# The first MLP's weight conversions on VectorE: whole tiles of 1024 columns, or halves of 512

## The chip, the cores and the metric

The kernel runs on one core of a Trainium2 chip. The metric is the device time of one execution in microseconds. The kernel before took 947.5 us, the median of three runs (946.28 to 948.18). The profiled execution took 947.39 us, of which the span from its first to its last instruction is 945.7 us.

## The reference

A causal attention over a window of 128 positions (4 sequences of 576 positions, 8 heads of 64, with a linear distance bias), and behind it two MLPs with different activations. All inputs and outputs are float32.

```python
scores = scale * np.matmul(q, k.transpose(0, 1, 3, 2))
rel = pos[:, None] - pos[None, :]
mask = (rel >= 0) & (rel < window)
scores = np.where(mask, scores + slopes * -abs(rel), -1e9)
attn = softmax(scores)
x = np.matmul(attn, v)                     # 2304 tokens x 512
h = x @ w_in1                              # 512 -> 2048
g = np.where(h >= 1, h, np.where(h <= -1, 0.0, (h + 1) ** 2 / 4))
x = g @ w_out1                             # 2048 -> 512
h = x @ w_in2
out = (h * np.clip(h + 3.0, 0.0, 6.0) / 6.0) @ w_out2
```

## The kernel before

Matmuls need more than one pass for float32 accuracy, so each operand is held as two parts, a high one and a low remainder, and each product is three matmuls (low x high, high x low, high x high).

The weights of both MLPs arrive as 64-bit floats. A tile of weights belongs to one slice f of 128 of the 2048 inner columns (f = 0 to 15) and holds, for 128 partitions, 512 columns of w_in and 512 of w_out: 1024 columns. To become float32 high and low parts it passes through six steps on three engines (the class `Weights`):

- `conv1`: ScalarE takes the magnitude of the upper words (line 194, tile `ma`), GpSimd clears what is not the sign in them (line 197, into `rawa`), ScalarE shifts the lower words (line 198, into `rawa`).
- `conv2`: VectorE shifts the magnitude and joins the sign (line 205), then adds the lower words as integers (line 212).
- `conv3`: ScalarE writes the high part (line 152, `wa<-ma`), VectorE the low part (line 159, `wa<-ma,wa`).

For the first MLP that is three VectorE instructions of 1024 columns for each of 16 slices. The names in the instruction order carry the slice: `ma3` and `wa3` belong to f = 3.

The attention runs in units of up to 256 positions, head by head, in steps: scores on TensorE into a bank `s` (line 411), the masked maximum on VectorE (line 441, `sm`), the exponential on ScalarE (line 445), transposes (lines 469, 470), values (line 506), the division on VectorE (lines 518 to 520, `y`), a transpose back (line 531), and the two parts of the MLP's input `x`: the high part on ScalarE (line 152), the low part on VectorE (line 159, `x<-x,x`). `x7` is the last pair of heads of the first unit.

The first MLP works on blocks of tokens: three of 256 and then wider ones of 384. For each slice f it makes `h` (12 matmuls, line 659, into one of two banks), the activation (VectorE line 688, ScalarE line 689, VectorE line 690, which ends the use of the bank), the two parts of `g` (ScalarE line 152, GpSimd line 159), and the second product into `acc` (12 matmuls, line 701), two slices behind. Blocks 0 and 1 go through slices 0 to 7 and then both through 8 to 15, so that the conversions, the loads and the attention's next units can run beside them. The conversions of w_in1 and w_out1 are spread over about the first 126 us. The second MLP has its own conversions (`mb`, `wb`), made around 500 to 570 us.

In this part of the program the order on SyncE (the DMA queue) is the order of the code; that of the four compute engines is set by a scheduler from the dependencies and the order of the code. Each engine then works through its list strictly in order.

Of the kernel before, what the change touches and what calls it, by code (L numbers as in the profile page):

```python
# [12 lines left out]
U32 = mybir.dt.uint32  # L13
I32 = mybir.dt.int32
U16 = mybir.dt.uint16
AF = mybir.ActivationFunctionType
ALU = mybir.AluOpType
# [23 lines left out]
def tile_window_attention_two_mlps(  # L41
# [15 lines left out]
    nc = tc.nc  # L57
# [92 lines left out]
    def split_hi(eng, hi, x):  # L150
        if eng == "act":
            nc.scalar.copy(hi, x)  # L152
        elif eng == "pool":
            nc.gpsimd.tensor_scalar(out=hi, in0=x, scalar1=1.0, scalar2=1.0, op0=ALU.mult, op1=ALU.mult)
        else:
            engines[eng].tensor_copy(hi, x)

    def split_lo(eng, lo, x, hi):
        engines[eng].tensor_tensor(out=lo, in0=x, in1=hi.bitcast(F32), op=ALU.subtract)  # L159
# [3 lines left out]
    class Weights:  # L163
# [36 lines left out]
        def conv2(self, f):  # L200


            raw, m = self.raw[f], self.m[f]
            if self.sign_pool:
                nc.vector.scalar_tensor_tensor(out=m.bitcast(U32), in0=m.bitcast(U32), scalar=3, in1=raw[..., 1],
                                               op0=ALU.logical_shift_left, op1=ALU.bitwise_or)
            else:
                nc.vector.tensor_scalar(out=m.bitcast(U32), in0=m.bitcast(U32), scalar1=3, scalar2=None,
                                        op0=ALU.logical_shift_left)
                nc.vector.scalar_tensor_tensor(out=m.bitcast(U32), in0=raw[..., 1], scalar=0x80000000,  # L210
                                               in1=m.bitcast(U32), op0=ALU.bitwise_and, op1=ALU.bitwise_or)
            nc.vector.tensor_tensor(out=m.bitcast(I32), in0=m.bitcast(I32), in1=raw.bitcast(I32)[..., 0], op=ALU.add)

        def conv3(self, f):
            del self.raw[f]
            m = self.m.pop(f)
            hl = wpool.tile([P, 2, 2, PIECE], F32R, tag=f"w{f}", name=f"w{self.nm}{f}")
            split_hi("act", hl[:, 0], m)
            split_lo("dve", hl[:, 1], m, hl[:, 0])
            self.hl[f] = hl  # L220

        def conv_tick(self):
# [618 lines left out]
    with ExitStack() as actx:  # L841
        mlp1 = Mlp1(W1, blocks1, rpool, gpool)
        raw = actx.enter_context(tc.tile_pool(name="raw", bufs=2))
# [92 lines left out]
    def tail_hook(f):  # L936
        if f >= LAG:

            W2.load()
            W2.load()  # L940
        if 4 <= f < 4 + 2 * KC:
            load_x2(xpool2, xs2, (f - 4) // KC, (f - 4) % KC)
        if f > LAG:
            with tc.issue_after(mlp1.square.ins), tc.issue_after(mlp1.larger.ins):
                conv2(0.5)
# [172 lines left out]
    def pair_hook(f, k):  # L1118
        if f == 0:
            W2.load()  # L1120
            W2.load()
        conv2(0.6)
        n = 2 * f + k
        if n == OWN - 1:
            assert not W2.conv_tick()
            xa.load(0)
            weight_sums(0)
            xa.make(0, temp_a)
            weight_sums(1)
            xa.make(1, temp_a)  # L1130
            weight_sums(2)
        if n == OWN + 3:
            xa.load(1)
        if n >= OWN:
            spare(1.3)
# [205 lines left out]
```

## Time and profile before

| what | value |
|---|---|
| median of 3 runs | 947.5 us |
| profiled execution | 947.39 us, span 945.7 us |
| TensorE busy | 929.6 us (98%) |
| VectorE busy | 661.1 us (70%) |
| ScalarE busy | 534.0 us (56%) |
| GpSimd busy | 305.9 us (32%) |

The shares are means over stages. In the page's row of 40 slices VectorE is at eight or nine tenths up to about 126 us and lower behind that, while TensorE is at nine tenths or more from about 50 us to the end. A busy TensorE is not TensorE at its peak, since its matmuls are pipelined. The granted clock is 1.000 of full speed over the whole span, the level of 2.4 GHz.

### The profile page before, as it was taken

Reading aid. Unit: us, or ns where it says so; the run is one execution under the profiler, and the core shown is the slowest. Engines: PE = TensorE matmul, PEld = TensorE weight load, DVE = VectorE, ACT = ScalarE, POOL = GpSimd, SP = SyncE. Lnnn points to the kernel's source line nnn. Section 1 sums busy time; section 2 is a strip of 40 time slices with the busy share of each in tenths; the row PEclk is TensorE's granted clock in tenths of the full one; section 3 lists DMA queues with packets and bytes.
Section 4 is the critical chain, followed back from the end, with each engine's and each line's share of the span. In section 5 each row is a group of like instructions: output and inputs, shape, how many; then the busy total and the mean of one; then the engine's idle time right before and its main releaser. Section 6 shows DMA issues by size and latency. Waiting matters only on the chain.

```text
span 945.7 us, 17240 instructions
## 1 busy us (share of the span) xinstructions
PE 929.6 (98%) x5683; PEld 875.8 (93%) x5683; DVE 661.1 (70%) x1750; ACT 534.0 (56%) x1349; POOL 305.9 (32%) x575
## 2 busy tenths in 40 slices
PE   8899999999999999999999999999999999999998
PEld 6799999999999999999999999999999898888987
DVE  5998975786677676767645999958557777644443
ACT  6998854676667566666634886535333334423233
POOL 3343854787668676767710000000000000000000
PEclk9999999999999999999999999999999999999999
DMA  9758332222212212222007861004264644544441
GB/s 263 233 168 262 112 99 88 68 81 72 73 54 82 72 52 62 80 84 56 7 34 249 304 235 59 1 23 167 79 211 166 236 170 147 170 124 114 122 113 67
DMA packets 95337, 114.90 MB, mean 122 GB/s; under 512 B 8848, under 2 KB 73616, under 8 KB 95248
## 3 DMA queue, kind: packets, MB, share of 16 engines
q1 hardware_dynamic: 95248, 113.80, 38.4%
q8 instruction: 45, 0.74, 0.3%
q14 instruction: 44, 0.36, 0.1%
HBM read 88.60 MB, written 25.17 MB: 120 GB/s over the span
## 4 chain that ended last, share of the span: by engine, by line
PE 86%; DVE 6%; DMA 3%; ACT 2%; issue 2%; POOL 0%; SPq 0%; ACTq 0%; POOLq 0%; DVEq 0%
PE h L659 25%; PE acc L760 21%; PE acc L701 17%; PE y L1242 7%; PE x L1242 5%; PE s L411 4%; PE r L554 3%; PE t L470 2%; PE r L506 1%; DMA rawa<-w_in 1%; DMA x2r<-x2d 1%; DVE r L688 1%; DMA kw<-kT 1%; DVE x L159 1%; DVE r L690 1%
## 5 line engine op out<-in xcount | busy, mean ns | idle before, releaser
L659 PE MATMUL h<-x,wa 128*128 128x384 f32 (+1 forms) x1344 | 231.0, 317 | 1.2 <-DVE r L690 0.8
L701 PE MATMUL acc<-g,wa 128*128 128x384 f32 (+1 forms) x1344 | 227.4, 315 | 0.4 <-POOL g L159 0.4
L760 PE MATMUL acc<-wb,g 128*128 128x512 f32 x861 | 222.2, 393 | 0.0
L659 PEld LDWEIGHTS h<-x,wa 128*128 128x128 f32 x1344 | 206.6, 189 | 4.4 <-DVE r L690 3.2
L701 PEld LDWEIGHTS acc<-g,wa 128*128 128x128 f32 x1344 | 206.2, 189 | 0.7 <-POOL g L159 0.6
L760 PEld LDWEIGHTS acc<-wb,g 128*128 128x128 f32 x861 | 159.4, 188 | 24.9
L152 ACT CAST g<-r 128x384 fp32r<-128x384 f32 (+1 forms) x208 | 101.3, 487 | 70.9 <-DVE r L1189 37.6
L159 POOL TENSOR_TENSOR g<-r,g 128x256 fp32r<-128x256 f32 (+1 forms) x96 | 92.9, 968 | 67.4 <-ACT g L152 54.3
L689 ACT ACTIVATE r<-r 128x384 f32<-128x384 f32 (+1 forms) x112 | 53.3, 478 | 82.9 <-DVE r L688 82.6
L159 DVE TENSOR_TENSOR g<-r,g 128x384 fp32r<-128x384 f32 x112 | 62.3, 557 | 41.9 <-ACT g L152 41.7
L688 DVE TENSOR_SCALAR r<-h 128x384 f32<-128x384 f32 (+1 forms) x112 | 55.4, 495 | 47.3 <-PE h L659 40.5
L488 POOL TENSOR_SCALAR_AFFINE_SELECT tt<-dist 128x256 fp32r<-128x256 f32 (+1 forms) x176 | 76.8, 457 | 14.1 <-DVE dist L483 13.9
L690 DVE TENSOR_TENSOR r<-h,r 128x384 f32<-128x384 f32 (+1 forms) x112 | 55.7, 499 | 29.7 <-ACT r L689 27.9
L659 PE MATMUL h<-x,wb 128*128 128x384 f32 x384 | 72.6, 336 | 0.0
L659 PEld LDWEIGHTS h<-x,wb 128*128 128x128 f32 x384 | 68.2, 188 | 2.6
L445 ACT ACTIVATE p<-p,sm 128x128 f32<-128x128 f32 (+2 forms) x134 | 56.9, 426 | 21.9 <-DVE sm L441 21.6
L1187 ACT ACTIVATE r<-u 128x384 f32<-128x384 f32 x32 | 16.8, 525 | 56.2 <-DVE u L1251 56.2
L554 PEld LDWEIGHTS r<-tt,vs 128*128 128x128 f32 x304 | 44.7, 189 | 3.5 <-issue 1.3
L393 POOL TENSOR_TENSOR qs<-qr,qs 128x256 fp32r<-128x256 f32 (+2 forms) x64 | 39.3, 616 | 25.0 <-ACT qs L390 13.3
L554 PE MATMUL r<-tt,vs 128*128 128x128 f32 (+3 forms) x304 | 44.3, 262 | 1.7 <-POOL tt L488 0.9
L391 DVE SCALAR_TENSOR_TENSOR kl<-kr,kh 128x256 fp32r<-128x256 f32 (+3 forms) x64 | 39.2, 613 | 0.0
L470 PE MATMUL t<-ident,p 128*128 128x128 f32 x134 | 38.4, 288 | 0.5 <-ACT tt L152 0.5
(161 smaller groups left out, 1554.3 us busy)
## 6 DMA issues: line engine op xcount, KB each, us to landing
w<-wd SPq DMA_DIRECT2D x88, 256.0 KB, 2.7
rawa<-w_in SPq DMA_DIRECT2D x16, 512.0 KB, 5.2
rawa<-w_out SPq DMA_DIRECT2D x16, 512.0 KB, 5.6
rawb<-w_in SPq DMA_DIRECT2D x16, 512.0 KB, 3.8
rawb<-w_out SPq DMA_DIRECT2D x16, 512.0 KB, 4.7
wd<-sum SPq DMA_DIRECT2D x32, 256.0 KB, 2.1
wd<-wb SPq DMA_DIRECT2D x24, 256.0 KB, 2.8
out<-o SPq DMA_DIRECT2D x17, 256.0 KB, 2.3
```

What stands on the lines that cost most here:

```text
L152: nc.scalar.copy(hi, x)
L159: engines[eng].tensor_tensor(out=lo, in0=x, in1=hi.bitcast(F32), op=ALU.subtract)
L445: nc.scalar.activation(out=pt[:, :nk], in_=pt[:, :nk], func=AF.Exp, bias=sm[:, 0:1], scale=-1.0, accum_out=None if u.whole else sm[:, 1:2])
L470: nc.tensor.transpose(ps[:, 1, :], pt[:, P:] if u.whole and has_prev else pt[:, :P], ident)
L488: nc.gpsimd.affine_select(out=u.tt[:, :, s0 + s, :m], in_=both, compare_op=ALU.is_ge, fill=0.0, base=-1 + s, pattern=[[0, 2], [sign, m]], ...
L554: nc.tensor.matmul(u.r[:, qo:qo + nq], u.vs[:, j, c, :, :].rearrange("p a d -> p (a d)"), u.tt[:, part].rearrange("p s q -> p (s q)")[:, s ...
L659: nc.tensor.matmul(ps[:, :n], self.W.w_in(a, c, f), self.x_chunk(x, b, c, n), start=(k == 0), stop=(k == 3 * KC - 1))
L688: nc.vector.tensor_scalar(out=r[:, :n], in0=ps[:, :n], scalar1=-1.0, scalar2=1.0, op0=ALU.max, op1=ALU.min)
L690: self.larger = nc.vector.tensor_tensor(out=r[:, :n], in0=ps[:, :n], in1=r[:, :n], op=ALU.max)
L701: nc.tensor.matmul(acc[i][:, o * n:(o + 1) * n], self.W.w_out(a, f)[:, e * P:(e + 1) * P], g[:, b, :n], start=(first and k == 0 and o == 0 ...
L760: nc.tensor.matmul(acc[t][:, :DM], g[:, b, tg * P:(tg + 1) * P], self.W.w_out(a, f), start=(first and k == 0), stop=(last and k == 2))
L1242: nc.tensor.matmul(ps[:, :N2], w[:, a, c * P:(c + 1) * P], self.x.operand(k, c, b), start=(start and n == 0), stop=(n == 5), skip_group_ch ...
```

## The change

For the first MLP (`sign_pool` is true for it alone) the three VectorE instructions of a slice become six: each works on 512 columns, k = 0 on the w_in half, k = 1 on the w_out half. The shift and the integer addition of one half stand next to each other in the code. ScalarE's and GpSimd's steps stay whole. The second MLP's conversions stay as they were (the branch is only turned round). Blocks, loads and the order of the DMA queue are the same, and 48 instructions are added in all.

```diff
             raw, m = self.raw[f], self.m[f]
             if self.sign_pool:
-                nc.vector.scalar_tensor_tensor(out=m.bitcast(U32), in0=m.bitcast(U32), scalar=3, in1=raw[..., 1],
-                                               op0=ALU.logical_shift_left, op1=ALU.bitwise_or)
-            else:
...
+                for k in range(2):
+                    nc.vector.scalar_tensor_tensor(out=m.bitcast(U32)[:, k], in0=m.bitcast(U32)[:, k], scalar=3,
+                                                   in1=raw[:, k, :, 1], op0=ALU.logical_shift_left, op1=ALU.bitwise_or)
+                    nc.vector.tensor_tensor(out=m.bitcast(I32)[:, k], in0=m.bitcast(I32)[:, k],
+                                            in1=raw.bitcast(I32)[:, k, :, 0], op=ALU.add)
+                return
...
             split_hi("act", hl[:, 0], m)
-            split_lo("dve", hl[:, 1], m, hl[:, 0])
+            if self.sign_pool:
+                for k in range(2):
+                    split_lo("dve", hl[:, 1, k], m[:, k], hl[:, 0, k])
+            else:
+                split_lo("dve", hl[:, 1], m, hl[:, 0])
```

In the changed kernel line 205 has become 206, line 212 has become 208, and lines from 222 on are 7 higher (688 is 695, 690 is 697, 441 is 448, 411 is 418, 659 is 666, 701 is 708, 520 is 527).

VectorE around the last input of the first block (`x7`), before; `r` is the activation of the first slice, `sm9_1` and `sm10_0` are maxima of the attention's second unit:

```order
L520 TENSOR_TENSOR y7_446<-r6_409,rec7_445 128x256
L441 ISA p1_114,sm9_1_489<-s9_1_487,dist_97 128x256
L441 ISA sm9_1_489 128x1
L205 SCALAR_TENSOR_TENSOR ma3_497<-ma3_497,rawa3_329 128x1024
L159 TENSOR_TENSOR x_78<-x7_475,x_78 128x256
L159 TENSOR_TENSOR wa2_494<-ma2_471,wa2_494 128x1024
L688 TENSOR_SCALAR r_514<-h_501 128x256
L212 ISA ma3_497<-rawa3_329,ma3_497 128x2048
L441 ISA p2_115,sm10_0_540<-s10_0_538,dist_97 128x256
```

The same place in the changed kernel:

```order
L527 TENSOR_TENSOR y7_449<-r6_412,rec7_448 128x256
L159 TENSOR_TENSOR wa1_473<-ma1_403,wa1_473 128x512 x2
L448 ISA p1_114,sm9_1_495<-s9_1_493,dist_97 128x256
L448 ISA sm9_1_495 128x1
L159 TENSOR_TENSOR x_78<-x7_481,x_78 128x256
L206 SCALAR_TENSOR_TENSOR ma2_477<-ma2_477,rawa2_261 128x512
L695 TENSOR_SCALAR r_523<-h_510 128x256
L208 ISA ma2_477<-rawa2_261,ma2_477 128x1024
L697 TENSOR_TENSOR r_523<-h_510,r_523 128x256
L206 SCALAR_TENSOR_TENSOR ma3_506<-ma3_506,rawa3_329 128x512 x2
L159 TENSOR_TENSOR wa2_502<-ma2_477,wa2_502 128x512 x2
L208 ISA ma3_506<-rawa3_329,ma3_506 128x1024 x2
```

The conversion of slice 3 has moved from in front of `x7` to behind the first activation; that of slice 2 has moved behind `x7`, and the maximum `sm10_0`, which follows the last row shown, now stands behind two more conversions.

TensorE a little later, where the first slice's products end and the attention's score `s10_1` follows, before:

```order
L659 MATMUL h_589<-x_78,wa1_468 128x256 x2
L506 MATMUL r8_480<-vr1_103,tt9_533 128x65 x4
L411 MATMUL s10_1_549<-kw1_106,qw0_107 128x256
L659 MATMUL h_671<-x_78,wa2_494 128x256 x12
L701 MATMUL acc0_721<-g_515,wa0_397 128x256 x5
```

In the changed kernel:

```order
L666 MATMUL h_601<-x_78,wa1_473 128x256 x3
L513 MATMUL r8_486<-vr1_103,tt9_545 128x65 x2
L708 MATMUL acc0_736<-g_524,wa0_399 128x256
L708 MATMUL acc1_737<-g_524,wa0_399 128x256
L708 MATMUL acc0_736<-g_524,wa0_399 128x256 x5
L666 MATMUL h_686<-x_78,wa2_502 128x256 x12
L708 MATMUL acc1_737<-g_524,wa0_399 128x256 x5
L418 MATMUL s10_1_561<-kw1_106,qw0_107 128x256
```

The score `s10_1` now stands behind slice 2's `h` and the whole second product of slice 0, where it stood ahead of both.

VectorE at the last conversion (slice 15), before:

```order
L212 ISA ma15_1771<-rawa15_1349,ma15_1771 128x2048
L688 TENSOR_SCALAR r_1824<-h_1811 128x256
L159 TENSOR_TENSOR x_78<-x29_1836,x_78 128x192
L438 COPY_PREDICATED s32_0_1847<-zeros_101,s32_0_1847 128x128
L441 ISA p0_113,sm32_0_1850<-s32_0_1847,zeros_101 128x128
L441 ISA sm32_0_1850 128x1
L159 TENSOR_TENSOR wa15_1833<-ma15_1771,wa15_1833 128x1024
L690 TENSOR_TENSOR r_1824<-h_1811,r_1824 128x256
```

In the changed kernel:

```order
L208 ISA ma15_1816<-rawa15_1379,ma15_1816 128x1024
L445 COPY_PREDICATED s32_0_1895<-zeros_101,s32_0_1895 128x128
L695 TENSOR_SCALAR r_1939<-h_1926 128x256
L448 ISA p0_113,sm32_0_1898<-s32_0_1895,zeros_101 128x128
L448 ISA sm32_0_1898 128x1
L398 SCALAR_TENSOR_TENSOR kl33_1906<-kr32_1543,kh33_1905 128x384
L159 TENSOR_TENSOR wa15_1880<-ma15_1816,wa15_1880 128x512 x2
L455 TENSOR_SCALAR sm32_0_1898<-sm32_0_1898 128x1
L697 TENSOR_TENSOR r_1939<-h_1926,r_1939 128x256
```

The end of the conversions has moved behind one activation more than before. From there on the four engines' lists are the same in both kernels.

## Rows read from the trace of the kernel before

**Rows 1.** Busy time in stretches (stretch: its length, busy us and count by engine)

```profile
25.00:35.00 10.00, 7.99 (x54) 6.84 (x55) 8.56 (x20) 9.05 (x18) 2.31 (x2) 1.00 0.87 249
35.00:62.00 27.00, 24.99 (x189) 23.29 (x188) 26.23 (x59) 25.31 (x49) 10.25 (x10) 1.00 0.52 166
62.00:95.00 33.00, 32.96 (x276) 32.41 (x275) 28.58 (x84) 29.61 (x68) 13.14 (x24) 1.00 0.81 258
95.00:126.00 31.00, 30.57 (x258) 30.30 (x257) 30.41 (x60) 25.59 (x56) 23.00 (x20) 1.00 0.36 111
```

**Rows 2.** Waits from 25 to 62 us (total us, times, longest)

```profile
PE s L411 <- DVE sm L441: 2.4, 3, 1.1
DVE ma L205 <- POOL rawa L197: 1.4, 3, 0.9
```

**Rows 3.** Timeline of VectorE, 31 to 39 us (start, duration, instruction, idle before)

```profile
31.50 1.20 DVE L212 CUSTOM_DVE_ANT_0 ma<-rawa,ma 128x2048 uint16<-128x2048 uint16 x1
32.61 0.42 DVE L520 TENSOR_TENSOR y<-r,rec 128x256 f32<-128x256 f32 x1
...
34.25 1.23 DVE L205 SCALAR_TENSOR_TENSOR ma<-ma,rawa 128x1024 uint32<-128x1024 uint32 x1 [0.88 <-POOL rawa L197]
35.39 0.42 DVE L159 TENSOR_TENSOR x<-x,x 128x256 fp32r<-128x256 f32 x1
35.73 1.22 DVE L159 TENSOR_TENSOR wa<-ma,wa 128x1024 fp32r<-128x1024 f32 x1
...
38.32 0.42 DVE L441 CUSTOM_DVE_ANT_0 p<-s,dist 128x256 f32<-128x256 f32 x1
```

**Rows 4.** Timeline of all engines around 34 us

```profile
33.04 1.17 POOL L197 TENSOR_SCALAR rawa<-rawa 128x1024 f32<-128x1024 f32 x1 [4.84 <-ACT ma L194]
...
34.20 0.37 ACT L152 CAST x<-x 128x256 fp32r<-128x256 f32 x1
...
35.86 0.51 PE L659 MATMUL h<-x,wa 128*128 128x256 f32 x2 [0.23 <-DVE x L159]
```

**Rows 5.** Timeline of TensorE, 38 to 41 us

```profile
38.80 0.70 PE L411 MATMUL s<-kw,qw 128*128 128x256 f32 x2 [1.09 <-DVE sm L441]
39.15 1.78 PE L659 MATMUL h<-x,wa 128*128 128x256 f32 x12
```

**Rows 6.** Timeline of VectorE around a 512-column copy, 121 us

```profile
121.49 0.68 DVE L156 COPY o<-acc 128x512 f32<-128x512 f32 x1
122.09 1.60 DVE L212 CUSTOM_DVE_ANT_0 ma<-rawa,ma 128x2048 uint16<-128x2048 uint16 x1
```

**Rows 7.** Conversions by form, 35 to 62 us (busy us, mean ns, idle before)

```profile
L205 DVE SCALAR_TENSOR_TENSOR ma<-ma,rawa 128x1024 uint32<-128x1024 uint32 x5 | 6.9, 1378 | 1.2 <-POOL rawa L197 1.2
L212 DVE CUSTOM_DVE_ANT_0 ma<-rawa,ma 128x2048 uint16<-128x2048 uint16 x4 | 5.9, 1463 | 0.0
L159 DVE TENSOR_TENSOR wa<-ma,wa 128x1024 fp32r<-128x1024 f32 x4 | 4.9, 1220 | 0.1
```

**Rows 8.** The same, 95 to 126 us

```profile
L159 DVE TENSOR_TENSOR wa<-ma,wa 128x1024 fp32r<-128x1024 f32 x5 | 7.6, 1512 | 0.0
L212 DVE CUSTOM_DVE_ANT_0 ma<-rawa,ma 128x2048 uint16<-128x2048 uint16 x5 | 7.4, 1475 | 0.0
L205 DVE SCALAR_TENSOR_TENSOR ma<-ma,rawa 128x1024 uint32<-128x1024 uint32 x5 | 7.1, 1428 | 0.1
```

**Rows 9.** Timeline of GpSimd, 103 to 107 us

```profile
103.88 0.73 POOL L159 TENSOR_TENSOR g<-r,g 128x256 fp32r<-128x256 f32 x1
...
106.66 1.69 POOL L159 TENSOR_TENSOR g<-r,g 128x256 fp32r<-128x256 f32 x1
```

**Rows 10.** Timeline of VectorE at the last conversion

```profile
124.80 1.23 DVE L159 TENSOR_TENSOR wa<-ma,wa 128x1024 fp32r<-128x1024 f32 x1
125.94 0.42 DVE L690 TENSOR_TENSOR r<-h,r 128x256 f32<-128x256 f32 x1
```

**Rows 11.** TensorE's line 659 alone: stretch, its length, busy us, count

```profile
0.00:137.06 137.06, 44.74 (x276) 1.00 0.64 194
```

More of the change, by code (lines that the diff above doesn't have):

```diff
@@ L204, in conv2 @@
             if self.sign_pool:
-                nc.vector.scalar_tensor_tensor(out=m.bitcast(U32), in0=m.bitcast(U32), scalar=3, in1=raw[..., 1],
-                                               op0=ALU.logical_shift_left, op1=ALU.bitwise_or)
-            else:
[L208 to L211, printed above, removed]
+                for k in range(2):
[4 more added lines that the diff above has]
+                return
+            nc.vector.tensor_scalar(out=m.bitcast(U32), in0=m.bitcast(U32), scalar1=3, scalar2=None,
+                                    op0=ALU.logical_shift_left)
+            nc.vector.scalar_tensor_tensor(out=m.bitcast(U32), in0=raw[..., 1], scalar=0x80000000,
+                                           in1=m.bitcast(U32), op0=ALU.bitwise_and, op1=ALU.bitwise_or)
             nc.vector.tensor_tensor(out=m.bitcast(I32), in0=m.bitcast(I32), in1=raw.bitcast(I32)[..., 0], op=ALU.add)
```

## The prediction

> **What bounds the kernel now.** I read the busy time in stretches first, since a mean over the span hides what differs between stages. TensorE is all but full from 35 us on: 24.99 of 27 us, then 32.96 of 33 and 30.57 of 31 [rows 1]. Behind the last conversion all four compute engines run the same lists in both kernels, so only what TensorE loses before about 126 us can change. From 25 to 62 us it loses 2.01 + 2.01 = 4.0 us, from 62 to 126 us 0.5 us. Before 25 us the order has hardly moved, and the loads are the limit there; I leave that stretch alone.
>
> The reader is to see in the same rows that VectorE is the second bound. It is busy 26.23 of 27 us from 35 to 62, and 30.41 of 31 from 95 to 126 [rows 1]. Between them, from 62 to 95 us, it has 4.4 us of idle time, and from 25 to 35 us 1.44. Then the waits say what TensorE's lost time is: 2.4 us for the attention's scores, which share one bank and wait for VectorE's maximum [rows 2]. VectorE itself loses 1.4 us in three waits of a conversion for GpSimd's step, 0.88 us of it at one place [rows 2, 3]. The timeline shows that place: a conversion of slice 3 stands at the head of VectorE's list and waits until GpSimd ends (33.04 + 1.17 = 34.21 us), with the low part of `x7` behind it. Its input was ready at 34.20 + 0.37 = 34.57 us, but it starts at 35.39, and TensorE's first `h` waits for it [rows 3, 4]. So a queue with a blocked head, not a lack of engine time, is what TensorE pays there.
>
> **The price of a half.** No conversion of 512 columns is in the trace. The nearest row is a copy of 512 columns: the instruction behind it starts 0.60 us after it [rows 6]. A whole conversion holds the queue 1.14 us (34.25 to 35.39) [rows 3]. So a split costs 2 x 0.60 - 1.14 = 0.06 us, and 48 of them 2.9 us. The other end is the sum by durations, as if nothing overlapped: 2 x 0.68 - 1.23 = 0.13 us, in all 6.2 us [rows 3, 6]. Below zero it can't be, since no column is dropped. I take 0.06, because the rows show the next instruction starting 0.08 to 0.09 us ahead of the end of a conversion (35.39 against 34.25 + 1.23) [rows 3], and in the changed list the shift and the addition of one half nearly always have another instruction between them.
>
> The Trainium skill, VectorE: DVE Perf Modes, section on the TRN2 errata, gives a float32 two-input instruction (N + 151)/0.96 ns; that is an estimate of 1224 ns for 1024 columns, which agrees with the mean of 1220 ns here [rows 7], and 691 ns for a half, 0.16 us per split. Its section on the DRAIN says that the next instruction does not start until the pipeline is empty; by that the 48 splits would hold the queue 7.5 us, and the sum below would come out slower. The starts in [rows 3] speak against the second rule; what is left of it is the slower rival below.
>
> **25 to 45 us, what moves.** In the changed list slice 3's conversion is behind the first activation, so `x7` no longer waits for it: 35.39 - 34.57 = 0.82 us. The attention's `y7` stands behind one half of slice 2's addition, not the whole one (31.50 to 32.61) [rows 3]: 1.11 - 0.60 = 0.51 us more. So `x7` and the first `h` come about 1.3 us earlier, `x7` near 34.1. But the work that was ahead of them is now behind them: two shifts, two low parts and two additions of slices 2 and 3 stand in one row ahead of the maximum `sm10_0`, 6 x 0.60 = 3.6 us. Behind `x7` come half a shift, the activation's first step, half an addition, its second step and these six; with 0.34 us for a step of 256 columns (35.39 to 35.73) that is 34.1 + 3 x 0.34 + 2 x 0.60 + 3.6 = 39.9 us, where `sm10_0` stood at 38.32 [rows 3]. The attention is thus late by 1.6 us where the MLP is early by 1.3. VectorE's own idle time is what is really saved: 0.88 us here and about 0.3 of the other waits for GpSimd, 1.2 us, which is the idle time that the grouped rows show ahead of the shifts [rows 7].
>
> TensorE can use that. Its 1.09 us wait for `s10_1`, behind which `h` of slice 2 was queued [rows 5], is now behind slice 2's `h` and slice 0's second product, 24 matmuls, of which twelve took 1.78 us [rows 5]; they fill the wait if slice 2's first half is there. The first half alone is enough for `h`, which gives back about 0.6 us of its later place. What is late next is the attention's score, by up to 1.6 us.
>
> **35 to 62 us, what it costs.** There are 5 + 4 + 4 = 13 conversions in the stretch [rows 7]: 13 x 0.06 = 0.8 us in a full queue, with no cover but the idle time just counted. Together: -1.2 + 0.8 = -0.4 us by 62 us. The splits from 25 to 35 us lie under VectorE's 1.44 us of idle time there; without that cover a half costs its 0.06 us there too.
>
> **62 to 126 us.** From 95 to 126 us there are 15 conversions [rows 8], 0.9 us against 0.6 us of idle time. All other splits, 48 - 13 - 15 = 20, make 1.2 us, and those of 62 to 95 us have 4.4 us of idle time to lie under: nothing. But a late conversion is not needed soon: the last low part ends at 126.03 us [rows 10], and TensorE starts the 24th `h`, the first with slice 15, after 276 matmuls of line 659, at 137.06 us [rows 11]. That is 11 us of cover. The activations stand in the same queue and have less of it, so I count 0 with an upper end of 15 x 0.13 = 2.0 us. Halves also change who holds up whom: a `g` low part on GpSimd takes 0.73 us, and 1.69 us beside a conversion, while the conversions of this stretch take 1428 to 1512 ns [rows 8, 9] against 1220 [rows 7]. The Trainium skill, SBUF — State Buffer, section Who interferes with whom, says that one of the two holds a shared port for its whole instruction and the other waits; the rows agree. By that rule a half lets GpSimd in up to 0.6 us sooner, and puts its 0.73 us ahead of the second half instead: the same time changes hands, and I count nothing.
>
> **The sum.** 947.39 - 0.4 = 947.0 us for the profiled execution, which lies 0.1 us under the median of 947.5. I take 947.0. Changes within 0.2%, 1.9 us either way of the median, cannot be told from none with these runs: faster begins below 945.6, slower above 949.4.
>
> **Rivals.** *Given back (the forecast, 946 to 949).* The lead turns into a late attention, and the time stays. For it speaks that VectorE is full from 35 to 62 us, so an order that serves one of its customers sooner serves the other later. If the scheduler keeps both halves side by side, as it does with 3 pairs in a row after `x7`, the halves act as whole tiles and the result is here too.
>
> *The lead is kept, 944.6.* TensorE's place is filled at once: the 1.3 us of `x7` and the 1.09 us wait in front of `s10_1` both go, and the saved queue time covers the splits: 947.39 - 1.3 - 1.09 - 0.4 for the sum above = 944.6. For it: from 25 to 62 us TensorE idles 4.0 us, so there is room. Against it: 3.6 us of conversions ahead of `sm10_0`, and later slices that are converted only shortly ahead of use.
>
> *VectorE becomes the bound, 949.6.* If a split costs 0.13 us, the two full stretches get (13 + 15) x 0.13 = 3.6 us more, against 0.8 + 0.6 us of idle time. The rest, 2.2 us, reaches TensorE through the maxima and the activations: 947.39 + 2.2 = 949.6. It decides from 0.05 us per split on, where the added time equals the idle time, and passes 949.4 near 0.12. For it: TensorE already waits for VectorE's maxima. Against it: the starts of rows 3.
>
> **Chances.** Given back 0.50, kept 0.26, VectorE the bound 0.24. The range of 944.3 to 950.3 takes in both rivals, the likeliest case's own is 945.6 to 949.0. Faster 0.26, same 0.50, slower 0.24.
>
> **What would show it.** A conversion of 512 columns should be followed after 0.60 us. VectorE's wait of 0.88 us for GpSimd ahead of a shift should be gone, `x7`'s low part should start near 34.1 us, and `sm10_0` near 39.9. TensorE's busy time from 25 to 62 us should rise by about half a microsecond, and that from 95 to 126 us should not fall by more than 0.5. The prediction is wrong if TensorE loses more than 5 us or less than 3 from 25 to 62, if the time moves before 25 us, or if a late slice's `h` waits for its conversion.

## The result and the profile after

The changed kernel takes 957.36 us (median of 957.50, 957.22, 958.32 and 955.24), the kernel before 946.89 us. The ratio is 1.0106, 95% interval 1.0085 to 1.0127: it is 10.5 us slower, where 947.0 was predicted and 950.3 was the upper end. The profiled execution took 957.5 us with a span of 955.8.

Line numbers of the changed kernel are 7 higher from L222 on (the attention's step L441 is L448, `y` L520 is L527); the shift L205 is L206, the addition L212 is L208.

The stretches answer to [rows 1] (length, then busy time and count of TensorE, its weight loads, VectorE, ScalarE, GpSimd, and the granted clock):

```profile
25.00:35.00 10.00, 8.97 (x62) 7.67 (x62) 9.55 (x24) 8.95 (x16) 2.45 (x2) 1.00 1.05 295
35.00:62.00 27.00, 23.44 (x158) 21.05 (x157) 24.71 (x61) 21.83 (x41) 8.78 (x8) 0.94 0.43 136
62.00:95.00 33.00, 31.97 (x261) 30.93 (x260) 30.77 (x95) 28.91 (x64) 9.50 (x22) 1.00 0.73 235
95.00:126.00 31.00, 27.84 (x230) 27.20 (x230) 30.75 (x67) 25.93 (x55) 18.88 (x21) 1.00 0.39 123
126.00:140.00 14.00, 14.00 (x108) 14.00 (x108) 12.20 (x32) 8.34 (x22) 5.23 (x8) 0.88 0.18 61
```

The counts tell more than the busy time. From 35 to 62 us TensorE runs 158 instructions where it ran 189, and from 95 to 126 us 230 instead of 258. Measured on the same group of twelve matmuls of the second product (L701, now L708), TensorE is 4.6 us late when the third of these groups ends (62.60 us against 57.99), 6.4 at the fifth, 4.7 again at the ninth, 5.4 at the fifteenth, 9.1 at the sixteenth, and 9.5 at the nineteenth (139.95 against 130.46). From there the lateness is constant for 350 us: nearly all that is lost is lost in two places.

The first place, on VectorE (start, duration; answers to [rows 3]):

```profile
33.30 0.42 DVE L159 TENSOR_TENSOR x<-x,x 128x256 fp32r<-128x256 f32 x1 [0.41 <-ACT x L152]
...
35.03 0.68 DVE L208 CUSTOM_DVE_ANT_0 ma<-rawa,ma 128x1024 uint16<-128x1024 uint16 x1
35.63 0.41 DVE L697 TENSOR_TENSOR r<-h,r 128x256 f32<-128x256 f32 x1
35.97 1.28 DVE L206 SCALAR_TENSOR_TENSOR ma<-ma,rawa 128x512 uint32<-128x512 uint32 x2
37.17 1.81 DVE L159 TENSOR_TENSOR wa<-ma,wa 128x512 fp32r<-128x512 f32 x2
38.91 2.21 DVE L208 CUSTOM_DVE_ANT_0 ma<-rawa,ma 128x1024 uint16<-128x1024 uint16 x2
41.04 0.41 DVE L448 CUSTOM_DVE_ANT_0 p<-s,dist 128x256 f32<-128x256 f32 x1
```

and beside it on GpSimd:

```profile
37.23 1.20 POOL L159 TENSOR_TENSOR g<-r,g 128x256 fp32r<-128x256 f32 x1 [2.99 <-ACT g L152]
38.41 1.59 POOL L197 TENSOR_SCALAR rawa<-rawa 128x1024 f32<-128x1024 f32 x1
```

A half alone is followed after 0.60 us (35.03 to 35.63), and the first pair takes 1.20. The next two pairs, which run beside GpSimd's two instructions, take 1.74 and 2.13 us. So `sm10_0` comes at 41.04 us, not at 38.32.

The second place is near 124 us; first VectorE, then TensorE:

```profile
120.10 1.90 DVE L206 SCALAR_TENSOR_TENSOR ma<-ma,rawa 128x512 uint32<-128x512 uint32 x2
121.92 1.23 DVE L159 TENSOR_TENSOR wa<-ma,wa 128x512 fp32r<-128x512 f32 x1
123.07 0.41 DVE L695 TENSOR_SCALAR r<-h 128x256 f32<-128x256 f32 x1
123.41 0.88 DVE L159 TENSOR_TENSOR wa<-ma,wa 128x512 fp32r<-128x512 f32 x1
...
125.36 0.41 DVE L527 TENSOR_TENSOR y<-r,rec 128x256 f32<-128x256 f32 x1
```

```profile
121.91 1.60 PE L666 MATMUL h<-x,wa 128*128 128x256 f32 x12
125.87 0.41 PE L513 MATMUL r<-vr,tt 128*128 128x65 f32 x2 [2.37 <-ACT vs L152]
```

The view names ScalarE's `vs` as the releaser of the 2.37 us wait, since it ends at 125.87 us. But the waiting matmul does not read `vs`, and in an experiment below (`normalise_first`) it starts at 123.41 us, while `vs` starts only at 126.03. What it waits for is `y`, which empties the bank `r` at 125.77 us.

Behind each place the granted clock falls: 0.68 from 45 to 50 us, after TensorE was busy 3.39 of the 5 us before, and 0.67 from 125 to 130, after 3.50 of 5. In each, some 3.3 us ran at 1.2 instead of 2.4 GHz; where TensorE has work all the time, that is an estimate of 1.6 us lost. In the kernel before the clock is 1.00 in all these stretches.

The conversions over the first 140 us, of the kernel before and of the changed one (busy us, mean ns of one, idle before):

```profile
L212 DVE CUSTOM_DVE_ANT_0 ma<-rawa,ma 128x2048 uint16<-128x2048 uint16 x16 | 21.7, 1355 | 0.0
L205 DVE SCALAR_TENSOR_TENSOR ma<-ma,rawa 128x1024 uint32<-128x1024 uint32 x16 | 21.3, 1334 | 1.5 <-POOL rawa L197 1.4
L159 DVE TENSOR_TENSOR wa<-ma,wa 128x1024 fp32r<-128x1024 f32 x16 | 21.0, 1311 | 0.4 <-ACT p L445 0.2
```

```profile
L206 DVE SCALAR_TENSOR_TENSOR ma<-ma,rawa 128x512 uint32<-128x512 uint32 x32 | 28.0, 881 | 0.0
L208 DVE CUSTOM_DVE_ANT_0 ma<-rawa,ma 128x1024 uint16<-128x1024 uint16 x32 | 27.3, 857 | 0.0
L159 DVE TENSOR_TENSOR wa<-ma,wa 128x512 fp32r<-128x512 f32 x32 | 22.1, 721 | 0.0
```

By means times counts that is 64.0 us before and 78.7 after: 14.7 more. At 0.68 us for an undisturbed half and 1.22 for a whole, 96 halves instead of 48 wholes explain 6.7; the other 8 us are longer durations than an undisturbed instruction has: waiting inside the instructions. The shift and the addition carry it, not the subtraction (721 ns).

### The profile page after: what moved, and what is told of

It is laid out like the page before. It is cut to its first block, busy times and chain, and to the rows that moved or that the text cites. A ratio compares the mean times of both kernels' runs of the same rounds, so it can differ in the third digit from the quotient of the medians.

```text
span 955.8 us, 17287 instructions
## 1 busy us (share of the span) xinstructions
PE 934.9 (98%) x5683; PEld 879.6 (92%) x5683; DVE 672.0 (70%) x1798; ACT 535.8 (56%) x1349; POOL 299.1 (31%) x575
## 4 chain that ended last, share of the span: by engine, by line
PE 87%; DVE 7%; ACT 2%; DMA 2%; issue 1%; POOL 0%; SPq 0%; ACTq 0%; DVEq 0%; POOLq 0%
PE h L666 25%; PE acc L767 21%; PE acc L708 17%; PE y L1249 7%; PE x L1249 5%; PE s L418 4%; PE r L561 3%; PE t L477 2%; PE r L513 1%; DVE ma L206 1%; DVE wa L159 1%; DVE ma L208 1%; DVE r L695 1%; DMA rawa<-w_out 1%; DVE kl L398 1%
## 5 line engine op out<-in xcount | busy, mean ns | idle before, releaser
L708 PE MATMUL acc<-g,wa 128*128 128x384 f32 (+1 forms) x1344 | 228.3, 317 | 1.5 <-POOL g L159 0.8
L708 PEld LDWEIGHTS acc<-g,wa 128*128 128x128 f32 x1344 | 207.1, 190 | 2.1 <-POOL g L159 1.0
L159 POOL TENSOR_TENSOR g<-r,g 128x256 fp32r<-128x256 f32 (+1 forms) x96 | 89.3, 930 | 70.7 <-ACT g L152 59.6
L1249 PE MATMUL y<-wb,w 128*128 128x384 f32 x192 | 38.7, 336 | 0.0
```

The lines of the kernel that those rows point to most:

```text
L708: nc.tensor.matmul(acc[i][:, o * n:(o + 1) * n], self.W.w_out(a, f)[:, e * P:(e + 1) * P], g[:, b, :n], start=(first and k == 0 and o == 0 ...
L1249: nc.tensor.matmul(ps[:, :N2], w[:, a, c * P:(c + 1) * P], self.x.operand(k, c, b), start=(start and n == 0), stop=(n == 5), skip_group_ch ...
```

## The experiments

Two theories. *Contact* (the expectations also call it price or port theory, and set a fixed-cost theory against it, by which a half costs some 0.07 us and nothing else): a VectorE instruction that meets one of GpSimd waits for it once, whatever its own length, so two halves wait twice. *Order*: the scheduler, given other lengths, puts the halves ahead of what TensorE needs. To part them, the issue order is pinned in some kernels: each engine's instructions are chained in a given order up to the tail part, and "old order" means that two halves stand where the whole stood.

```
+    for engine, n in (...):
+        ins = [i for i in nc.cur_bb.bb.instructions if i.engine == engine]
+        for a, b in zip(own, own[1:]):          # own: the order wanted
+            tc.add_manual_dep(ins[b], ins[a].name, ...NoSync...)
```

All medians are in us, beside 947.0 to 947.2 for the kernel before on the same chip. The kernel before was not run with its own order pinned; a pinned kernel below takes 945.7, so no large cost of the pinning is to be seen.

**Halves in the old order** (the pinning added to the changed kernel).

> All 96 halves, but every engine issues in the order of the kernel before (each pair of halves stands where the whole instruction stood). Order theory (the loss of 10.5 us comes from where the scheduler puts the halves and what they push back): the order is the old one, so 946.5 to 949.5 us, TensorE's granted clock stays 1.0. Price theory (halves cost VectorE time wherever they stand: 48 x 0.07 = 3.4 us of fixed cost and some 8 us of waiting for GpSimd): 953 to 958 us, VectorE's conversions held some 70 us against 60.8 before. If both act, between 950 and 953.

Measured 952.3, ratio 1.0053 [1.0036, 1.0069]. Between the two, as expected if both act: half of the loss is there without the new order. It builds up slowly (TensorE is 1.4 us late at the third group, 2.1 at the ninth, 4.4 at the nineteenth), the clock stays at 1.00, and the durations of the conversions are 77.0 us. VectorE is what is full:

```profile
35.00:62.00 27.00, 24.49 (x178) 22.11 (x177) 26.59 (x68) 24.19 (x48) 8.38 (x9) 1.00 0.49 154
62.00:95.00 33.00, 32.93 (x270) 31.92 (x269) 30.32 (x95) 29.36 (x66) 12.91 (x24) 1.00 0.80 255
95.00:126.00 31.00, 28.93 (x238) 28.12 (x237) 31.00 (x67) 25.07 (x53) 17.70 (x19) 1.00 0.36 110
```

**Wholes in the new order** (the kernel before, pinned; the whole stands where the first half stood, then where the last one stood).

> The 48 whole conversions of the kernel before, but every engine issues in the order of the changed kernel (a whole conversion stands where its first half stood). Order theory: 954 to 958 us, with TensorE's two stalls near 40 to 45 and 120 to 126 us and the granted clock at half behind them. Price theory: 946 to 949 us.

> 48 whole conversions, sign and all, every engine in the order of the changed kernel, with a whole conversion where its last half stood (the earlier run with wholes in this order put them where the first half stood and ended at 958.75 us). Order theory: 950 to 953 us, since what was ahead of the attention's step is less now. If the place of the whole does not matter: 957 to 960 us.

Measured 958.75, ratio 1.0121 [1.0100, 1.0142], and 960.75, ratio 1.0136 [1.0115, 1.0158]. The new order is a bad one for whole tiles, in either place. How much of the changed kernel's loss it makes can't be read from this: the first of the two was 4.5 us late at its first `h` already (28.25 us against 23.78; the changed kernel 1.8), and the second missed its expectation by 8 us.

**Part of the conversions** (two kinds, then half of the slices; the scheduler free).

```
             split_lo("dve", ...)  whole             # shift_add_halves
             shift and addition    whole             # subtract_halves
+            if self.sign_pool and f >= 8:           # late_slices; early_slices: f < 8
```

> Only the shift and the addition (L206, L208) are in halves, 64 of the 96; the subtraction is whole; the scheduler orders anew. Price theory: about two thirds of the loss, 953 to 955 us. Order theory: any value between 946 and 958, given by whether VectorE's order puts halves ahead of the attention's step near 38 to 41 us; if it does, the loss up to 60 us is the 5 us of the changed kernel.

> Only the subtraction is in halves, 32 of the 96; shift and addition are whole; the scheduler orders anew. Price theory: about a third of the loss, 949.5 to 951.5 us. Order theory: any value between 946 and 958, by the order near 38 to 41 and 120 to 126 us.

> Halves only for weight slices 8 to 15 (24 conversions in 48 halves). Price theory: TensorE is not late until 75 us, then about half of the 5.2 us that halves cost in the old order: 949 to 950 us. Order theory: the new order near 120 to 126 us comes with it, 4 us more: 951 to 954 us.

> Halves only for weight slices 0 to 7 (24 conversions in 48 halves). Price theory: about half of the 5.2 us, 949 to 950 us. Order theory: the early loss of the changed kernel, 5 us by 95 us, and no more after: 951.5 to 953 us.

Measured 952.3, 952.37, 949.98 and 952.89, with ratios of 1.0053 [1.0037, 1.0070], 1.0052 [1.0036, 1.0069], 1.0028 [1.0017, 1.0039] and 1.0055 [1.0039, 1.0072]. Sixteen splits of the subtraction cost as much as 32 of the others, so a price per split alone is wrong; with the subtraction split, TensorE's clock fell too (0.94 from 35 to 62 us). The late slices alone cost 2.8 us and left TensorE on time until 107 us; the early ones cost 5.7. None is better than whole tiles.

**The price by itself.** No part of the kernel is left in this one.

> Leaves out the whole computation: VectorE's subtractions (whole: 1024 columns; or two halves of 512) are run in sets of 16, with GpSimd idle, with GpSimd running the sign step (1024 columns, in place) without pause, and with GpSimd running the subtraction of g (256 columns) without pause; also with one instruction that reads a PSUM bank behind each whole or pair, or between the halves. Fixed-cost theory (a half costs 0.07 us more than half a whole and nothing else): a pair of halves takes 1.2 us against 1.13 for a whole in every set, so the sets with GpSimd differ by 1 to 2 us of 18 to 20. Port theory (VectorE and GpSimd take turns on SBUF, one instruction each, so a pair of halves waits twice where a whole waits once): with GpSimd idle 1.2 against 1.13; beside the sign step a pair takes at least 0.5 us more than a whole; with a PSUM instruction between the halves more is lost or gained by whether that instruction lets GpSimd in.

Four of its sets: wholes and halves with GpSimd idle, then beside the sign step (here L74). The two rows in timeline form are VectorE from inside the last two sets, where GpSimd does not pause:

```profile
L64 DVE TENSOR_TENSOR lo<-m,hi 128x1024 f32<-128x1024 f32 x16 | 19.6, 1225 | 0.5
...
L67 DVE TENSOR_TENSOR lo<-m,hi 128x512 f32<-128x512 f32 x32 | 19.4, 678 | 0.0
...
L64 DVE TENSOR_TENSOR lo<-m,hi 128x1024 f32<-128x1024 f32 x16 | 30.2, 1890 | 0.5
L74 POOL TENSOR_SCALAR sign<-sign 128x1024 f32<-128x1024 f32 x15 | 29.2, 1946 | 1.2
...
L74 POOL TENSOR_SCALAR sign<-sign 128x1024 f32<-128x1024 f32 x20 | 28.2, 1410 | 1.6
```

```profile
59.13 12.08 DVE L64 TENSOR_TENSOR lo<-m,hi 128x1024 f32<-128x1024 f32 x6
...
93.54 11.96 DVE L67 TENSOR_TENSOR lo<-m,hi 128x512 f32<-128x512 f32 x8
```

Alone, a pair takes 1.21 us (19.37 us for 16 pairs) and a whole 1.26 from start to start. Beside the sign step a whole takes 12.08 / 6 = 2.0 us and a half 11.96 / 8 = 1.5: each gives way to one GpSimd instruction and pays about the same for it, 0.8 us a whole and 0.9 a half. So a pair takes 3.0 us and a split costs 1.0, not 0.06. GpSimd gains by it: its step, 1.09 us alone, falls from 1946 to 1410 ns. An instruction with one input in PSUM, between or behind the halves, took 0.41 us in every set, undisturbed, and was free beside the sign step: a whole and such an instruction together take 2.02 us from start to start, the whole by itself as much. Beside `g`'s subtraction a whole took 1.58 us and a half 1.17 on the mean. The Trainium skill, SBUF — State Buffer, section Who interferes with whom, has two rules: a VectorE instruction with two SBUF inputs contends with a GpSimd instruction that reads SBUF, and the order of issue decides who blocks. The sets agree with the first; for the second they show that the two engines block each other in turn.

**The sign step taken away**, once with wholes and once with halves in the old order, once with halves in the new order.

```
-                sign = raw.bitcast(F32)[..., 1]
+                sign = raw.bitcast(F32)[:, 0, :2, 1]
-                ... in1=raw[..., 1], op0=ALU.logical_shift_left
+                ... in1=no_sign.to_broadcast([P, 2, PIECE]), op0=ALU.logical_shift_left
```

> Leaves out the weights' sign: GpSimd's sign step (L197) covers 2 columns instead of 1024, and the shift (L205) takes a zero in its place; whole conversions, all orders as in the kernel before. Port theory: VectorE's 48 conversions take 3 to 5 us less than the 64.0 us of the kernel before in durations, and the end is 945 to 947 us (a part of VectorE's waits is on no path). Fixed-cost theory: VectorE's durations stay within 1 us.

> The same without the sign, with 96 halves in the order of the kernel before. It is read against the run with whole conversions and no sign. With the sign step, halves in the old order took 13.0 us more in VectorE's durations and cost 5.2 us at the end. Port theory: most of the 13.0 is waiting for GpSimd, of whose work the sign step is the longest instruction, so the difference falls to 7 to 9 us in durations and to 2 to 3.5 us at the end. Fixed-cost theory: the difference at the end stays at 5.2 us.

> Leaves out the weights' sign as before (sign step on 2 columns); 96 halves, all engines in the order of the changed kernel. With the old order and no sign the end was 946.4 us. Order theory (the changed kernel's order costs some 5 us by itself, beside 5 us of waiting for the sign step): 950.5 to 952.5 us. Contact theory (the order costs only because halves wait for GpSimd in it): 946 to 948 us.

Measured 945.68, 946.36 and 948.87, ratios 0.9985 [0.9973, 0.9996], 0.9989 [0.9978, 1.0000] and 1.0018 [1.0007, 1.0030]. Halves in the old order now cost 0.7 us more than wholes instead of 5.2, within what the intervals leave open, and in the profiled executions TensorE ends the third, ninth and nineteenth group 0.5, 0.3 and 0.1 us earlier with halves than with wholes. Their conversions:

```profile
L209 DVE CUSTOM_DVE_ANT_0 ma<-rawa,ma 128x1024 uint16<-128x1024 uint16 x32 | 22.4, 739 | 0.0
L207 DVE SCALAR_TENSOR_TENSOR ma<-ma,const-float32-0.0 128x512 uint32<-128x512 uint32 x32 | 22.2, 734 | 0.0
L159 DVE TENSOR_TENSOR wa<-ma,wa 128x512 fp32r<-128x512 f32 x32 | 21.7, 718 | 0.2
```

The means of the shift and the addition fall from 830 and 867 ns (old order, with the sign step) to 734 and 739. The shift also reads a constant here instead of the sign words; the addition's operands are the old ones, and it falls as well. So the loss in the old order needs the sign step, and the cost of the added starts hides in VectorE's idle time: from 35 to 126 us that falls from 7.4 us with wholes to 4.8 with halves, and TensorE is not later. Two things are not separated: by durations the halves take 13.0 us more than the wholes with the sign step and still 9.1 more without it (70.1 against 61.0), so 3.9 us of them go with that step, and its absence also leaves VectorE more idle time in which the rest can hide (7.4 us with wholes, where the kernel before has 5.8). The new order costs 948.87 - 946.36 = 2.5 us without the sign step and 957.4 - 952.3 = 5.1 with it: neither theory's number. The order has a price of its own, and contact doubles it. Without the sign step TensorE loses 0.3 us between the ninth and the nineteenth group in the new order, where the changed kernel loses 4.8: the late loss goes with the sign step, and what is the order's own stands ahead of the ninth group.

**The sign step in halves too**, with wholes and with halves, old order.

> 48 whole conversions in the order of the kernel before; GpSimd's sign step is two instructions of 512 columns instead of one of 1024. Port theory: what a VectorE instruction loses in a contact is about one GpSimd instruction, so the contacts are shorter and there are more of them: 945.5 to 947.5 us, a gain of at most the 1.3 us that leaving out the sign gave. Fixed-cost theory: no change, within 0.5 us of the kernel before.

> 96 halves on VectorE in the order of the kernel before, and GpSimd's sign step in two instructions of 512 columns. With whole sign steps this ended at 952.3 us. Port theory: each contact of a half with a sign step costs about half as much, so about half of the 5.2 us comes back: 949 to 950.5 us. Fixed-cost theory: 952 to 953 us.

Measured 949.35, ratio 1.0015 [1.0002, 1.0027], and 951.48, ratio 1.0038 [1.0027, 1.0049]. Shorter GpSimd instructions don't help wholes, which lose some 2.3 us where neither theory said more than 0.5. Halves end 0.8 us earlier than beside whole sign steps, with intervals that overlap; the port theory's "half" is not borne out. Against wholes with the same sign steps the halves cost 2.1 us, not 5.2. That the number of contacts counts here, and not their length alone, would fit, but no run shows it.

**The head pinned, and two moves at the late place.**

> All 96 halves; the four compute engines issue in the order of the kernel before (halves where the whole stood) up to 45 us, and as the scheduler likes from there. If the new order at the head (six halves of slices 2 and 3 ahead of the attention's step) makes the early loss of 4.6 us at 60 us, TensorE is at most 1.5 us late at 60 us and its clock is not halved at 45 us; the end is then 951 to 954 us (price 5 of it). If it does not matter, 956 to 958 us.

Measured 956.17, ratio 1.0096 [1.0081, 1.0111]. TensorE is about 1.1 us late after the second group and 1.5 at the fifth, so the early loss is indeed the order's; but its clock fell from 40 to 45 us all the same (0.75), and 6.3 us were lost later, in other waits of the free part and with a second fall of the clock (0.71 from 125 to 130 us). Only 1.2 us came back.

```
  VectorE near 120 us, as in the changed kernel:  L206 x2, L159, L695, L159, L697, L525, L448, L526, L398, L527
  normalise_first:  L525, L526, L527, L206 x2, ...   attention_first:  L525, L448, L526, L527, L206 x2, ...
```

> The changed kernel with every engine's order as it is there, but for one move on VectorE: the three instructions that normalise head pair 28/29 (L525, L526, L527: rec and y, 0.72 us, which ended at 125.77 us) stand ahead of the four halves that began at 120.10 us instead of behind them. Order theory: TensorE's 2.37 us wait at 123.5 us for the bank that y empties is gone or under 0.5 us, its clock stays at 1.0 there, and the end comes 3.5 to 4.2 us earlier: 953 to 954 us. If VectorE's amount of work is what binds there, TensorE waits for the activation behind the halves instead and the end comes less than 1.5 us earlier: 956 to 957.5 us.

> As the run in which the normalisation stood ahead of the four halves near 120 us, but with the attention's step p of head 31 (L448, 0.34 us) ahead of them too; that run had TensorE wait 1.68 us at 125.6 us for this p, behind the four halves, where it had waited 2.37 us for y in the changed kernel, and ended at 955.73 us. Order theory: the four halves (4.1 us long) then hold up nothing that TensorE needs next, the wait falls under 0.4 us, and the end is 953.3 to 954.6 us. If VectorE's amount of work is the bound there, the same time is lost in the next wait: 955.4 to 957 us.

Measured 955.73, ratio 1.0089 [1.0065, 1.0113], and 955.45, ratio 1.0091 [1.0071, 1.0111]. TensorE's waits from 119 to 140 us (total, times, longest), first with `y` ahead, then with both ahead:

```profile
PE s L418 <- DVE sm L448: 2.2, 2, 1.7
```

```profile
PE s L418 <- DVE sm L448: 1.3, 2, 0.9
PE acc L708 <- DVE o L156: 0.3, 1, 0.3
```

The 2.37 us wait became one of 1.68 behind the same four halves; with that one removed too, TensorE started the sixteenth group 2.8 us earlier than in the changed kernel and ended the nineteenth only 1.6 us earlier, and most of the rest went into the next waits for VectorE. The clock stayed at 1.00 there in both. So the greater part of the late loss is VectorE's amount of work, in line with the 0.3 us without the sign step; the order decides in how large a lump TensorE feels it, and behind the large lump the clock fell as well. The order theory's 953 to 954.6 us did not come.

## Why the prediction was wrong, by its steps

*The bound.* Right: TensorE full, VectorE next. The rival "VectorE becomes the bound" named the right engine and place, 35 to 62 and 95 to 126 us, at 949.6, with another cause: a higher price of a start, not waits for GpSimd.

*The price of a half.* 0.06 us is right for a half alone (0.60 us to the next start, 16 pairs in 19.37 us). "Below zero it can't be" is too strong: with GpSimd idle, and nothing between them, the 16 pairs took less than the 16 wholes (1.21 against 1.26 us each). Without the sign step all 96 halves in the old order cost 0.7 us at the end.

*"The same time changes hands, and I count nothing"* is the first step that failed. GpSimd does get in sooner, as said, and its sign steps fall from 1407 to 1251 ns (first 140 us, before and after):

```profile
L197 POOL TENSOR_SCALAR rawa<-rawa 128x1024 f32<-128x1024 f32 x16 | 22.5, 1407 | 40.8 <-ACT ma L194 31.3 <-DMA qw<-qT 9.5
```

```profile
L197 POOL TENSOR_SCALAR rawa<-rawa 128x1024 f32<-128x1024 f32 x16 | 20.0, 1251 | 47.6 <-ACT ma L194 38.1 <-DMA qw<-qT 5.3 <-DMA kw<-kT 4.3
```

But VectorE is the engine on the path and GpSimd is not, so time that passes from one to the other is a loss. And it isn't the same time: each half can wait for a GpSimd instruction of its own, 1.0 us per split when GpSimd does not pause, some 8 us more over the 96 halves than over the 48 wholes. In the old order the halves cost 5.2 us at the end, 0.7 without the sign step. My reason for not counting it was that a long conversion makes GpSimd wait; that its length protected VectorE from a second wait I did not see. A hint was there: 1512 ns for the low part where GpSimd is busy longer, against 1220 [rows 7, 8]. That this is a price per instruction and not per column, to be multiplied by the instructions, only the sets without the kernel show (0.8 us a whole, 0.9 a half).

*25 to 45 us, the -1.2 us,* is the second step that failed. `x7` came even earlier than forecast (33.30 us, not 34.1), and the 0.88 us wait went. `sm10_0` was 1.1 us later than forecast (41.04, not 39.9), because the six halves ahead of it took 5.07 us and not 3.6. The sum took VectorE's idle time of 1.2 us as saved; from 25 to 62 us VectorE idled 2.74 us instead of 2.21, so nothing was saved. Nor did slice 0's second product fill TensorE's wait of 1.09 us: it waited itself for `g` on ScalarE and GpSimd, the score still waited 0.96 us for VectorE, and TensorE's clock fell behind these gaps.

```profile
37.20 0.50 PE L708 MATMUL acc<-g,wa 128*128 128x256 f32 x2 [0.67 <-ACT g L152]
38.49 0.86 PE L708 MATMUL acc<-g,wa 128*128 128x256 f32 x5 [0.79 <-POOL g L159]
...
44.13 0.70 PE L418 MATMUL s<-kw,qw 128*128 128x256 f32 x2 [0.96 <-DVE sm L448]
```

The net of -0.4 us by 62 us was +4.6. By the same third group it is +1.4 in the old order, and in the new order without the sign step +2.2, where the old order without it stands at -1.5: the reordering, which the prediction counted as a gain, is a loss of 3 to 4 us at this place in the profiled executions and of 2.5 (without the sign step) to 5.1 us (with it) at the end.

*The test that I set* was half blind: TensorE's busy time from 25 to 62 us fell by 0.57 us instead of rising by 0.5, and it lost 4.6 us, inside the 3 to 5 that I allowed, while TensorE was 4.6 us late. Where the clock has fallen, fewer matmuls fill the same busy time: three matmuls of `h` in a row start 0.21 us apart at 47.5 us, at 1.2 GHz, and 0.12 us apart at 49.5, at 2.4. The counts show it. Two other signs did speak: TensorE's busy time from 95 to 126 us fell by 2.7 us, and its first `h` started at 25.57 us, not at 23.78, so the order had moved before 25 us as well.

*62 to 126 us.* The 11 us of cover of the late conversions were not what mattered: the activations, of which the prediction says that they have less, `y` and the scores stand in the same queue. The upper end of 2.0 us was too low for the first reason above; 4.8 us were lost between the ninth and the nineteenth group, 2.4 in the old order, 0.3 in the new order without the sign step.

The 2.5 us that the new order costs without the sign step are not the clock's: it fell in the profiled execution (0.79 from 35 to 40 us, 0.87 from 40 to 45), but in six of the ten executions its mean was 1.000, and their median is 948.9 us as well. What stays open is which of TensorE's gaps make them, and why wholes in this order lose more than halves.

## What to carry to other kernels

Before splitting an instruction, ask whom it meets: here VectorE's wait for GpSimd was paid per instruction and not per column (0.8 us a whole, 0.9 a half). Time that "changes hands" between two engines is a loss where only one of them is on the path. Compare TensorE's counts and clock, not its busy time alone, and pin the issue order once to tell a price from a reordering.

## What the runs showed of the hardware

VectorE and GpSimd alternate one instruction each when both are always ready, with two SBUF inputs on VectorE and the sign step on GpSimd: half and sign step both started every 1.5 us, whole and sign step every 2.0. Instructions with one PSUM input kept their 0.41 us beside the same GpSimd work, and fitted into VectorE's wait. TensorE's clock fell to 1.2 GHz behind 5 us with 3.39 and 3.50 us of work in the changed kernel; with the halves in the old order it stayed at 2.4 behind 5 us with 3.04 (25 to 30 us), so the amount of work alone does not tell when it falls.
